# The first S1 group behind the parameter transposes, and whole copies of X chunk 0

## Chip, cores and metric

The kernel runs on one core of one Trainium2 chip. The metric is the device time of one execution in microseconds (us). Most executions of a kernel agree within 0.3%.

## What is computed

A gated mix of two branches over x (2048 tokens, 1024 features, bf16). Cut to what matters:

```python
g = sigmoid((x * gate_w).sum(-1, keepdims=True))
# branch A: a diagonal complex state space model
dt = exp(log_dt); Lam_bar = exp(dt * Lam)
B_bar = ((Lam_bar - 1.0) / Lam)[:, None] * Bmat
h[t] = Lam_bar * h[t-1] + x[t] @ B_bar.T          # over all 2048 tokens
a = 2.0 * real(h @ Cmat.T) + x * Dskip
# branch B: the 8 tokens with the largest x @ w_r go through a gated MLP
b = x + scatter_add(mlp(x_sel) * sigmoid(r_sel))
out = g * a + (1 - g) * b
```

Only the start of branch A is touched by the change: the projection of x by B, and the small parameters (log_dt, Lambda) from which tables of sines and cosines are made.

## The kernel before

**Stages.** Tokens are cut into 8 chunks of 256 (LC); X[m] holds two chunks transposed, features on the partitions. S1 is the projection by B: for each pair of chunks m and each of 8 blocks ct of 128 states, a real and an imaginary group of 8 matmuls accumulate over the features into one PSUM tile "vps" (`s1u`, line 159), and ScalarE evacuates it to V in two casts (`s1e`, line 274, instruction at line 279). There are two vps tiles, so the group (m, ct + 2) needs the evacuation of (m, ct). VectorE turns V by the tables, scans along the tokens and turns back to H (`dve_m`, `dve_scan`, `dve_post`), and S2 multiplies H by C into the output (`s2`, line 757). The MLP of branch B is cut into slots that are put between the S1 and S2 groups.

**Order.** TensorE, VectorE, ScalarE and SP (the queue of most loads) each run their instructions in the order in which the program writes them; the tile framework puts in the semaphore waits. So the order of the lines of the kernel's first part is the order on each engine.

**Loads.** SP's queue issues the first token tile of x (token rows 0 to 127) as it is, then B's first real column block (128 states), x chunk 1 transposed, B's first imaginary block, and the other blocks of B, all transposed by DMA (`load_B`, `load_xT`). ScalarE's queue issues the second token tile (rows 128 to 255), then the three rows log_dt, Lambda_re and Lambda_im into `vrow` (line 85). Chunk 0 of x is not transposed by a DMA but on TensorE: per token tile 8 transposes into the PSUM tile `xq`, and copies from there into X[0] (lines 168 to 174).

**The first part on TensorE, in order.** `warm(12)`: 12 matmuls of zeros (256 columns) into a PSUM tile that nobody reads; the 16 transposes of x chunk 0; `warm(2)`; the first S1 group, `s1u(0, 0, 0, 0, 1)`: state block 0, real part, chunk 0 alone, 8 matmuls of 256 columns; three transposes of the parameter rows into `va_ps` (line 179); `warm(2)`; `s1u(0, 0, 0, 1, 2)`, the same for chunk 1; `s1u(0, 0, 1, 0, 2)`, the imaginary part of both chunks, 8 matmuls of 512 columns; two transposes of the rows w_r and gate_w (line 435); then `s1(0, 1)`, `s1(0, 2)` and so on, 16 matmuls of 512 columns each.

**The parameter chain.** VectorE casts va_ps to `vec` (line 180); ScalarE makes dt_b by an exponential (194); VectorE makes the angles (197) and are (199), ScalarE rdec (201); VectorE makes the arguments of the tables (`tab_arg`, lines 222, 223 and 225, and `tab_abs`, 230); ScalarE the sines and cosines nTi and T2tab (236, 237), three small operations on the angles (393 to 396), and only then the evacuation of state block 0 (279), since `s1e(0, 0)` is written behind them. After it come copies of d0 and two more sines (249, 250), the evacuation of state block 1, and so on.

Lines of the page: L152 is a warm matmul, L164 an S1 matmul, L171 a transpose of x chunk 0, L174 the copies into X[0], L179 the transposes of the parameter rows, L279 the evacuation of V, L298 to L300 the multiplies and adds of `dve_m`, L766 and L782 the S2 matmuls.

Of the kernel before, what the change touches and what calls it, by code (L numbers as in the profile page):

```python
# [10 lines left out]
F32 = mybir.dt.float32  # L11
# [5 lines left out]
P = 128  # L17
LC = 256
# [6 lines left out]
def kernel(  # L25
# [19 lines left out]
    nc = tc.nc  # L45
# [4 lines left out]
    KD = D // P  # L50
# [16 lines left out]
    ps_s1 = ctx.enter_context(tc.tile_pool(name="ps_s1", bufs=2, space=PSUM))  # L67
# [3 lines left out]
    X = {}  # L71
    BT = [const.tile([P, KD, NP_], BF16, name=f"BT{pl}", tag=f"BT{pl}") for pl in range(2)]
# [43 lines left out]
    def big_new(name, k, shape=None, dt=BF16):  # L116
        want = {"V": "H", "U": "U", "H": "V", "D": "V"}[name]
        pick = next((e for e in big_free if e[1] == want), big_free[0])
        big_free.remove(pick)
        big_tag[name, k] = pick[0]  # L120
        return const.tile(shape or [P, 2, NCT, LC], dt, name=name, tag=pick[0])
# [28 lines left out]
    def warm(n):  # L150
        for _ in range(n):
            nc.tensor.matmul(wps[:], lhsT=wt0[:, 0:P], rhs=wt0[:], start=True, stop=True)  # L152

    V = {}
    H = {}

    vp = {}

    def s1u(m, ct, pl, k0, k1):
        if (m, ct) not in vp:  # L160
            vp[m, ct] = ps_s1.tile([P, 2, 2, LC], F32, name="vps", tag="vps")
        o = vp[m, ct][:, pl, k0:k1, :].rearrange("p k t -> p (k t)")
        for dc in range(KD):
            nc.tensor.matmul(o, lhsT=BT[pl][:, dc, ct * P:(ct + 1) * P], rhs=X[m][:, dc, k0 * LC:k1 * LC], start=(dc == 0), stop=(dc == KD - 1))  # L164

    warm(12)
    vec = small.tile([P, 3, NCT], F32, name="vec")
    for tl in range(BPC):
        xq = ps_s2.tile([P, KD, P], BF16, name="xq", tag="zps")
        for dc in range(KD):  # L170
            nc.tensor.transpose(xq[:, dc, :], x0r[:, tl, dc * P:(dc + 1) * P], ident[:])  # L171
        for h, copy in enumerate((nc.vector.tensor_copy, nc.scalar.copy)):
            hs = slice(h * KD // 2, (h + 1) * KD // 2)
            copy(out=X[0][:, hs, tl * P:(tl + 1) * P], in_=xq[:, hs, :])  # L174
    warm(2)
    s1u(0, 0, 0, 0, 1)
    va_ps = ps_m.tile([P, 3, NCT], BF16, name="va_ps", tag="m")
    for i in range(3):
        nc.tensor.transpose(va_ps[:, i, :], vrow[:, i, :], ident[:NCT, :NCT])  # L179
# [59 lines left out]
    def tab_neg(q):  # L239
        cs = slice(q * QC, (q + 1) * QC)  # L240
        nc.vector.tensor_scalar(out=T2tab[:, 1, cs, :], in0=T2tab[:, 0, cs, :], scalar1=-1.0, scalar2=None, op0=ALU.mult)
# [23 lines left out]
    def tab_bwd_b(q):  # L265
        C32, q1, q2 = tabs.pop(q)
        for c in range(QC):
            ct = q * QC + c
            nc.vector.scalar_tensor_tensor(out=Ctab[:, ct, :], in0=C32[:, c, :], scalar=c2r[:, ct:ct + 1], in1=q1[:, c, :], op0=ALU.mult, op1=ALU.add)
            nc.vector.scalar_tensor_tensor(out=S2tab[:, 1, ct, :], in0=C32[:, c, :], scalar=c2i[:, ct:ct + 1], in1=q2[:, c, :], op0=ALU.mult, op1=ALU.add)  # L270
        cs = slice(q * QC, (q + 1) * QC)
        nc.vector.tensor_scalar(out=S2tab[:, 0, cs, :], in0=S2tab[:, 1, cs, :], scalar1=-1.0, scalar2=None, op0=ALU.mult)

    def s1e(m, ct):
        for kk in range(2):
            k = 2 * m + kk
            if k not in V:
                V[k] = big_new("V", k)
            nc.scalar.copy(out=V[k][:, :, ct, :], in_=vp[m, ct][:, :, kk, :])  # L279
        vp.pop((m, ct))  # L280

    def s1(m, ct):
        for pl in range(2):
            s1u(m, ct, pl, 0, 2)
        s1e(m, ct)
# [4 lines left out]
    def bc(ap, c0, c1):  # L290
        return ap[:, c0:c1, :].unsqueeze(1).to_broadcast([P, 2, c1 - c0, LC])

    def dve_m(k, c0, c1):
        v = V[k][:, :, c0:c1, :]
        if c0 == 0:
            G[k] = big_new("U", k)
        u = G[k][:, :, c0:c1, :]
        nc.vector.tensor_tensor(out=u, in0=v, in1=T2tab[:, :, c0:c1, :], op=ALU.mult)  # L298
        nc.vector.tensor_tensor(out=v, in0=v, in1=bc(nTi, c0, c1), op=ALU.mult)  # L299
        nc.vector.tensor_tensor(out=u, in0=u, in1=V[k][:, ::-1, c0:c1, :], op=ALU.add)  # L300
        if c1 == NCT:
            big_done("V", k)
        if k > 0:
            nc.vector.tensor_tensor(out=u[:, :, :, 0], in0=u[:, :, :, 0], in1=rst[k - 1][:, :, c0:c1], op=ALU.add)
# [21 lines left out]
    def dve_p(k, c0, c1, i):  # L326
        if c0 == 0 and i == 0:
            H[k] = big_new("H", k)
        h = H[k][:, :, c0:c1, :]
        g = G[k][:, :, c0:c1, :]  # L330
# [41 lines left out]
    def last_post(hf, c0, c1):  # L372
        k = NK - 1
        if hf == 0 and c0 == 0:
            H[k] = big_new("H", k)
        ts = slice(hf * P, (hf + 1) * P)
        h = H[k][:, :, c0:c1, ts]
        g = G[k][:, hf, :, c0:c1]
# [17 lines left out]
    nc.scalar.activation(out=trig[:, 0], in_=aab[:], func=ACT.Sin, scale=-TWO_PI, bias=halfpi[:])  # L396

    tab_neg(0)
    warm(2)
    s1u(0, 0, 0, 1, 2)  # L400
    s1u(0, 0, 1, 0, 2)
    s1e(0, 0)
# [43 lines left out]
    tab_bwd_q(0, 2, 4)  # L446
    s1(0, 3)
    tab_bwd_b(0)
    dve_m(0, 2, 4)
    dve_scan0(0, 2, 4)  # L450
# [16 lines left out]
    dve_scan0(0, 6, 8)  # L467
    dve_state(0, 4, 8)
    tab_bwd_b(1)
    dve_post(0, 0, 8)  # L470

# [285 lines left out]
    def s2(b, dh):  # L757
# [6 lines left out]
        for ct in range(NCT):  # L764
            for pl in range(2):
                nc.tensor.matmul(zps[:], lhsT=H[k][:, pl, ct, tl * P:(tl + 1) * P], rhs=CT[pl][:, ct, dsl], start=(fresh and ct == 0 and pl == 0), stop=(ct == NCT - 1 and pl == 1), skip_group_check=not fresh)  # L766
        if dh == 1 and tl == 1:
# [126 lines left out]
    for n, (m, k) in enumerate(blocks):  # L894
        free_w.extend(fill.get(n, ()))
        if n == 7:
            for pl in range(2):
                t = const.tile([P, 4, 2, D], BF16, name="wdb", tag=f"BT{pl}")
# [48 lines left out]
```

## Time and profile before

| what | value |
|---|---|
| median of 3 runs | 248.49 us (248.42 to 248.64) |
| profiled execution, time | 248.64 us |
| its span in the profile | 246.9 us |
| granted TensorE clock, mean | 1.00 |
| first token tile of x landed, transposes of x start on TensorE | 4.34, 4.35 us |
| first S1 matmul | 6.75 us |
| parameter rows transposed (va_ps) | 7.89 us |
| vec | 8.16 us |
| first evacuation of V starts | 14.51 us |
| third S1 pair of groups, s1(0, 2), starts | 15.61 us |
| first S2 matmul in the chain | 66.40 us |
| last S2 matmul ends | 243.66 us |

The span is the time from the first to the last record of the profile; the time of the execution holds it and 1.74 us besides. Starts are counted from the span's start. PE is TensorE's matmuls, PEld its weight loads, DVE is VectorE, ACT ScalarE, POOL GpSimd, SP SyncE; a q behind a name is the engine's queue of DMA issues. In a timeline a row has the start, the length, the engine, the line, the operation, the output and input, and in brackets the idle time of the engine ahead of it and what ended that. Matmuls are pipelined, so a row of several is longer than their spacing times their number.

### The profile page before, as it was taken

The numbers are of one execution on the slowest core, as the hardware profiler recorded it, in microseconds if no ns is written. First come the engines' busy times: TensorE is split into PE (matmuls) and PEld (weight loads), VectorE is DVE, ScalarE is ACT, GpSimd is POOL, SyncE is SP. The second block draws the span as 40 slices with busy tenths as digits, with TensorE's granted clock in tenths as the row PEclk, the third lists the DMA queues.
The fourth block names the chain that finished last, engine by engine and source line by source line (L and its number), as shares of the span: only waits on it lengthen the run. The fifth ranks groups of instructions, "written<-read, shape, count | busy, mean of one in ns | idle before, by whom it ended". The sixth has DMA issues, their size and how long they took to land.

```text
span 246.9 us, 3503 instructions
## 1 busy us (share of the span) xinstructions
PE 239.6 (97%) x1354; PEld 112.8 (46%) x1378; DVE 225.9 (92%) x230; ACT 119.2 (48%) x206; POOL 26.8 (11%) x47
## 2 busy tenths in 40 slices
PE   7989999999999999999999999999999999999994
PEld 5534444444444444444444444444444444446453
DVE  0679999999999999999999999999999999999952
ACT  2499994333372563233365472135267445456421
POOL 4000000000000300720002021100000211110210
PEclk9999999999999999999999999999999999999999
DMA  7899999999860270476247989777599999962052
GB/s 185 200 202 200 214 241 208 212 231 262 284 208 0 66 191 0 74 175 212 96 165 221 347 231 353 236 258 279 179 333 303 390 311 305 81 146 39 2 131 85
DMA packets 65313, 48.48 MB, mean 196 GB/s; under 512 B 50560, under 2 KB 52224, under 8 KB 65296
## 3 DMA queue, kind: packets, MB, share of 16 engines
q1 hardware_dynamic: 59968, 37.20, 56.8%
q0 software_dynamic: 3264, 7.38, 14.7%
q10 hardware_dynamic: 2064, 3.68, 4.4%
q8 instruction: 11, 0.18, 0.3%
q14 instruction: 6, 0.05, 0.1%
HBM read 27.55 MB, written 8.40 MB: 146 GB/s over the span
## 4 chain that ended last, share of the span: by engine, by line
PE 93%; DVE 2%; ACT 2%; DMA 1%; issue 1%
PE vps L164 42%; PE zps L766 42%; PE zps L782 3%; PE pgu L658 3%; DMA x0r<-in_A_x_dram 1%; PE y L670 1%; PE xq L171 1%; PE zr L484 1%; DVE tf L225 1%; DVE tu L222 0%; ACT nTi L236 0%; ACT T2tab L237 0%; ACT V L279 0%; DVE tu L223 0%; DVE ot L787 0%
## 5 line engine op out<-in xcount | busy, mean ns | idle before, releaser
L164 PE MATMUL vps<-X,BT 128*128 128x512 bf16 (+1 forms) x508 | 111.7, 376 | 1.7 <-ACT V L279 0.9
L766 PE MATMUL zps<-CT,H 128*128 128x512 bf16 x469 | 104.4, 379 | 0.6
L164 PEld LDWEIGHTS <-BT 128*128 128x128 bf16 x520 | 50.3, 98 | 61.4 <-issue 2.6
L766 PEld LDWEIGHTS <-H 128*128 128x128 bf16 x480 | 46.5, 98 | 56.6 <-issue 1.3
L309 DVE TENSOR_TENSOR_SCAN U<-d,U 128x2048 bf16<-128x2048 f32 (+2 forms) x22 | 62.0, 2859 | 0.6
L279 ACT CAST V<-vps 128x512 bf16<-128x512 f32 x64 | 34.3, 587 | 57.5 <-PE vps L164 55.1
L771 ACT ACTIVATE ot<-zps,gcol 128x512 bf16<-128x512 f32 x30 | 20.6, 686 | 46.1 <-PE zps L766 44.9
L740 ACT CAST zps<-xd 128x512 f32<-128x512 bf16 (+1 forms) x29 | 16.6, 576 | 3.8 <-ACT xt L727 3.3
L299 DVE TENSOR_TENSOR V<-V,nTi 128x4096 bf16<-128x4096 bf16 (+2 forms) x11 | 16.7, 1516 | 0.5
L298 DVE TENSOR_TENSOR U<-V,T2tab 128x4096 bf16<-128x4096 bf16 (+2 forms) x11 | 16.6, 1509 | 0.5
L300 DVE TENSOR_TENSOR U<-U,V 128x4096 bf16<-128x4096 bf16 (+2 forms) x11 | 16.7, 1516 | 0.4
L336 DVE TENSOR_TENSOR H<-H,U 128x4096 bf16<-128x4096 bf16 x7 | 16.0, 2292 | 0.2
L334 DVE TENSOR_TENSOR U<-U,S2tab 128x4096 bf16<-128x4096 bf16 x7 | 16.0, 2292 | 0.2
L792 POOL DMA_DIRECT2D out_dram<-ot x14 | 13.0, 926 | 29.3 <-ACT ot L771 27.3
L704 POOL DMA_DIRECT2D xt<-in_A_x_dram x12 | 7.1, 595 | 82.5 <-DMA out_dram<-xt 36.8
L727 ACT ACTIVATE xt<-xt,omgcol 128x1024 bf16<-128x1024 bf16 x14 | 16.0, 1144 | 0.0
L332 DVE TENSOR_TENSOR H<-U,Ctab 128x4096 bf16<-128x4096 bf16 x7 | 16.0, 2285 | 0.0
L367 DVE TENSOR_TENSOR_SCAN U<-D,U 128x1024 bf16<-128x1024 f32 x4 | 8.9, 2279 | 0.1
L722 DVE TENSOR_TENSOR xd<-xt,Dbc 128x1024 bf16<-128x1024 bf16 x14 | 9.0, 684 | 0.0
L658 PE MATMUL pgu<-wgu,xsel 128*32 128x448 bf16 x128 | 7.2, 354 | 0.1
L782 PE MATMUL zps<-CT,H 128*128 128x256 bf16 (+1 forms) x47 | 7.1, 306 | 0.1
L717 POOL DMA_DIRECT2D out_dram<-xt x2 | 1.5, 754 | 49.2 <-ACT zps L740 49.2
(152 smaller groups left out, 128.3 us busy)
## 6 DMA issues: line engine op xcount, KB each, us to landing
wgu<-in_B_w_gate_dram SPq DMA_DIRECT2D x16, 448.0 KB, 3.6
wgu<-in_B_w_up_dram SPq DMA_DIRECT2D x16, 448.0 KB, 5.7
out_dram<-ot POOLq DMA_DIRECT2D x14, 256.0 KB, 6.4
wdb<-in_B_w_down_dram SPq DMA_DIRECT2D x7, 512.0 KB, 10.7
xt<-in_A_x_dram POOLq DMA_DIRECT2D x12, 256.0 KB, 4.0
out_dram<-xt ACTq DMA_DIRECT2D x12, 256.0 KB, 5.0
wd<-in_B_w_down_dram SPq DMA_DIRECT2D x5, 512.0 KB, 9.9
xt<-in_A_x_dram SPq DMA_DIRECT2D x4, 256.0 KB, 3.3
```

The lines of the kernel that those rows point to most:

```text
L164: nc.tensor.matmul(o, lhsT=BT[pl][:, dc, ct * P:(ct + 1) * P], rhs=X[m][:, dc, k0 * LC:k1 * LC], start=(dc == 0), stop=(dc == KD - 1))
L279: nc.scalar.copy(out=V[k][:, :, ct, :], in_=vp[m, ct][:, :, kk, :])
L298: nc.vector.tensor_tensor(out=u, in0=v, in1=T2tab[:, :, c0:c1, :], op=ALU.mult)
L299: nc.vector.tensor_tensor(out=v, in0=v, in1=bc(nTi, c0, c1), op=ALU.mult)
L300: nc.vector.tensor_tensor(out=u, in0=u, in1=V[k][:, ::-1, c0:c1, :], op=ALU.add)
L309: nc.vector.tensor_tensor_scan(out=fl, data0=d0[:, c0:c1, :].rearrange("p c t -> p (c t)"), data1=fl, initial=0.0, op0=ALU.mult, op1=ALU.add)
L332: nc.vector.tensor_tensor(out=h, in0=g, in1=bc(Ctab, c0, c1), op=ALU.mult)
L334: nc.vector.tensor_tensor(out=g, in0=g, in1=S2tab[:, :, c0:c1, :], op=ALU.mult)
L336: nc.vector.tensor_tensor(out=h, in0=h, in1=G[k][:, ::-1, c0:c1, :], op=ALU.add)
L740: nc.scalar.copy(out=z[:], in_=xd[b][:, d_:d_ + w])
L766: nc.tensor.matmul(zps[:], lhsT=H[k][:, pl, ct, tl * P:(tl + 1) * P], rhs=CT[pl][:, ct, dsl], start=(fresh and ct == 0 and pl == 0), stop= ...
L771: nc.scalar.activation(out=ots[b][:, dsl], in_=zps[:], func=ACT.Copy, scale=gcol[:, b:b + 1])
```

## The change

Two things change; nothing else in the program does.

1. Each token tile of chunk 0 was copied from PSUM into X[0] in two halves, features 0 to 511 by VectorE and 512 to 1023 by ScalarE. Now ScalarE copies the whole of token tile 0, and VectorE the whole of token tile 1.
2. The first S1 group moves on TensorE from ahead of the transposes of the parameter rows to behind them, with one more warm matmul ahead of it. In the program it stands behind `tab_neg(0)`, but no TensorE instruction lies between the parameter transposes and that place, so on TensorE the order is: warm(2), va_ps, warm(1), the first S1 group, warm(2), and on as before. The definition of `s1u` is moved down with it, which has no instruction of its own.

```diff
     warm(12)
     vec = small.tile([P, 3, NCT], F32, name="vec")
     for tl in range(BPC):
         xq = ps_s2.tile([P, KD, P], BF16, name="xq", tag="zps")
         for dc in range(KD):
             nc.tensor.transpose(xq[:, dc, :], x0r[:, tl, dc * P:(dc + 1) * P], ident[:])
-        for h, copy in enumerate((nc.vector.tensor_copy, nc.scalar.copy)):
-            hs = slice(h * KD // 2, (h + 1) * KD // 2)
-            copy(out=X[0][:, hs, tl * P:(tl + 1) * P], in_=xq[:, hs, :])
+        (nc.scalar.copy if tl == 0 else nc.vector.tensor_copy)(out=X[0][:, :, tl * P:(tl + 1) * P], in_=xq[:])
     warm(2)
-    s1u(0, 0, 0, 0, 1)
     va_ps = ps_m.tile([P, 3, NCT], BF16, name="va_ps", tag="m")
...
     tab_neg(0)
+    warm(1)
+    s1u(0, 0, 0, 0, 1)
     warm(2)
     s1u(0, 0, 0, 1, 2)
     s1u(0, 0, 1, 0, 2)
```

More of the change, by code (lines that the diff above doesn't have):

```diff
@@ L152, in warm @@
             nc.tensor.matmul(wps[:], lhsT=wt0[:, 0:P], rhs=wt0[:], start=True, stop=True)
[L154 to L164, printed above, removed]
     warm(12)
@@ L272, in tab_bwd_b, with s1u @@
         nc.vector.tensor_scalar(out=S2tab[:, 0, cs, :], in0=S2tab[:, 1, cs, :], scalar1=-1.0, scalar2=None, op0=ALU.mult)
+    V = {}
+    H = {}
+    vp = {}
+    def s1u(m, ct, pl, k0, k1):
+        if (m, ct) not in vp:
+            vp[m, ct] = ps_s1.tile([P, 2, 2, LC], F32, name="vps", tag="vps")
+        o = vp[m, ct][:, pl, k0:k1, :].rearrange("p k t -> p (k t)")
+        for dc in range(KD):
+            nc.tensor.matmul(o, lhsT=BT[pl][:, dc, ct * P:(ct + 1) * P], rhs=X[m][:, dc, k0 * LC:k1 * LC], start=(dc == 0), stop=(dc == KD - 1))
     def s1e(m, ct):
```

## The prediction

> **What bounds the kernel now.** I read the busy shares first, then the chain of work that ended last, then the waits of TensorE, then the first 24 us instruction by instruction. The first two lines are from the page: TensorE and VectorE are both busy nearly all the time, and the chain is nine tenths TensorE.
>
> ```profile
> PE 239.6 (97%) x1354; PEld 112.8 (46%) x1378; DVE 225.9 (92%) x230; ACT 119.2 (48%) x206; POOL 26.8 (11%) x47
> PE 93%; DVE 2%; ACT 2%; DMA 1%; issue 1%
> ```
>
> So the 2% on VectorE and the 2% on ScalarE are the part of the chain in which TensorE doesn't set the pace. The chain in order of time (start, length, what) shows that they lie in one place, the first 16 us:
>
> ```profile
> 6.27 0.43 DVE X L174
> ...
> 7.36 0.60 PE vps L164 x4
> 7.96 0.17 PE va_ps L179 x3
> 8.13 0.02 issue
> 8.16 0.20 DVE vec L180
> ...
> 14.61 0.96 ACT V L279 x2
> 15.57 0.04 issue
> 15.61 5.45 PE vps L164 x24
> ```
>
> The parameter chain starts with the transposes of the Lambda rows (va_ps), goes over vec, the tables and the sines, and ends with the first evacuation of V on ScalarE (L279), which frees the PSUM tile that the third S1 group needs. From 15.61 us on the chain is TensorE without a break. The waits of TensorE have one entry there (total, times, longest):
>
> ```profile
> PE vps L164 <- ACT V L279: 0.9, 1, 0.9
> ```
>
> So whatever starts the parameter chain earlier moves all that follows, until TensorE's own queue is the later of the two. The timeline gives the pieces (start, length):
>
> ```profile
> 5.42 0.42 DVE L174 COPY X<-xq 128x512 bf16<-128x512 bf16 x1 [4.41 <-PE xq L171]
> 5.88 0.58 ACT L174 COPY X<-xq 128x512 bf16<-128x512 bf16 x1 [2.10 <-DVE X L174]
> 6.03 0.63 PE L152 MATMUL wps<-wt 128*128 128x256 bf16 x2
> 6.27 0.42 DVE L174 COPY X<-xq 128x512 bf16<-128x512 bf16 x1 [0.43 <-PE xq L171]
> 6.73 0.58 ACT L174 COPY X<-xq 128x512 bf16<-128x512 bf16 x1 [0.27 <-DVE X L174]
> 6.75 1.21 PE L164 MATMUL vps<-X,BT 128*128 128x256 bf16 x8
> 7.89 0.23 PE L179 MATMUL va_ps<-ident,vrow 8*128 8x8 bf16 x3
> ```
>
> The first S1 group stands ahead of va_ps on TensorE. It waits for both engines' copies of X, the second ScalarE copy ending at 7.31, and so holds va_ps back to 7.89.
>
> **The change, part by part.** (1) The copies of X chunk 0. Four half copies go (two on VectorE of 0.42, two on ScalarE of 0.58, each of which starts only when VectorE's half of the same tile is done); one whole copy on each engine comes. VectorE's whole copy (1024 elements) has no row. Its bounds are 0.42 and twice that, 0.85. The multiplies of L298 took 0.69 at 1024 elements and 2.29 at 4096, so 0.521 ns per element and 0.156 us fixed; at 512 elements this line gives 0.42, which is the copy's own row, so I take 0.69. ScalarE's whole copy lies between the sine L236 at 1024 elements, 1.06, and two halves, 1.17; I take 1.1. ScalarE may start when VectorE now starts its first half, 5.42, and ends by 6.6. VectorE starts at 6.27 as now (token tile 1 is transposed then) and ends at 6.96, at most 7.12. ScalarE's copy costs nothing, being hidden behind VectorE's by 0.35 us; ScalarE's next work, dt_b, needs vec.
>
> (2) va_ps directly behind the two warm matmuls. These start at 6.03 and 6.24, 0.21 apart, so TensorE is free at 6.45. vec began 0.27 after va_ps's first transpose; that makes about 6.8 with the pause of 0.09 that now stands ahead of va_ps. VectorE is then still in the X copy to 6.96, so vec starts at about 6.99 in place of 8.16: **1.17 us earlier** (1.0 with the copy at 0.85). No DMA is moved, but TensorE reads the rows 1.4 us earlier than now, and their landing isn't shown. The rows ride on ScalarE's queue (q10). Its packets in the windows 4.8 to 5.0 and 5.0 to 5.2 us (packets, MB, share) are the last, none comes from 5.2 to 5.4:
>
> ```profile
> q10 hardware_dynamic: 3, 0.00, 1.4%
> ...
> q10 hardware_dynamic: 1, 0.00, 0.3%
> ```
>
> The same queue's x0r landed at 4.54 (issue 0.74 plus 3.8), some 0.75 to 0.95 after its last large packets near 3.6 to 3.8. By that the rows are there at 5.95 to 6.15, before 6.45. From above the landing is bounded by 7.89, when they are read today without a wait on a DMA.
>
> (3) The first S1 group, now behind va_ps and one more warm matmul. The warm matmul takes 0.11 to 0.21 and lies in the wait for VectorE's copy: nothing; without that wait it would cost its length. The group starts 0.06 after VectorE's copy (as 6.69 to 6.75 now): 7.02. Eight matmuls of 256 columns at 0.107 apart make 7.88; the two warm ones took 0.23 with what follows (8.05 to 8.28): 8.11; the second half, 0.86: 8.97. The imaginary group then needs B's imaginary column block, issued at 5.50 and landed 3.5 later, at 9.0; it began at 9.15 before. So TensorE is 0.10 to 0.15 **ahead** of now, though the group moved behind other work: its own copies come at 6.96 in one piece where they came at 6.69 and 7.31. The pair of groups that follows, (0,1), has 16 matmuls of 512 columns from 11.11 on, 0.215 apart (six steps from 9.37 to 10.66 before it), so it leaves TensorE free at 14.55 now and at about 14.45 afterwards.
>
> (4) What is late next. The chain from vec to L279 has no other input that comes late: the table load follows rdec, the ramp was made at 1.3, and the matmuls that L279 reads are done before 11. So L279 ends at 15.56 - 1.17 = 14.39, and the third pair starts at the later of 14.39 + 0.05 and 14.45: **14.45 for 15.61, 1.16 us earlier**. ScalarE and TensorE then arrive within 0.05 of each other, so any further delay of TensorE in the first 14 us is now paid for. With VectorE's copy at 0.85 it is 1.0; I take 1.1. Behind this point the next meeting is the second evacuation (18.06 to 19.12) with the fourth pair (15.61 + 3.45 = 19.06): both move by the same. VectorE, which waits only 0.9 us for T2tab between vec and the last block, moves by 1.17 too. SP's transposes do not move. The tightest is B imaginary, columns 4 and 5, landed at 17.09 + 5.6 = 22.7; it is read at 19.17 + 3.45 + 1.72 = 24.3 now and 23.2 afterwards, 0.5 to spare. The last two X chunks are issued from 50.43 on in 4.22 us; by the 4.9 us that an earlier one took, the second lands near 57.5, and the gate rows read it at 60.7 now, 59.5 afterwards.
>
> The sum: span 246.9 - 1.1 = 245.8, plus the 1.74 that lie outside the span in the profiled execution (248.64), makes 247.54. That execution is 0.15 above the median of the runs shown, 248.49; against the median it is **247.4 us**, 0.44% less.
>
> [...] Row: the warm matmuls at 6.03 and 6.24 are 0.21 apart, the S1 matmuls from 6.75 on 0.107, so TensorE goes to full speed in between, after 2.4 us of work since 4.35, and the profile's granted clock of 1.0 throughout doesn't show it. [...]
>
> **Rivals.** *The clock comes late* (slower). Place: TensorE between 6.45 and 7.02, where a dense S1 group is replaced by three tiny transposes, a warm matmul and a short pause. Full speed later by t costs t/2, and TensorE has no slack left, so it decides from t/2 = 1.16. [...] Against it: the pause of 0.54 ahead of 4.35 was longer, and only some 0.1 to 0.3 us of work is missing.
>
> *The rows come late* (no change). If they land only near 7.85, va_ps runs when it does today, vec and L279 stay, and TensorE, with two groups behind va_ps, is free at 15.5, just ahead of 15.61: 248.4 us. For it: no row shows the landing; against it: the last packet at 5.2. A landing between gives part of the gain.
>
> *Hidden later.* The gain is real at 14.45 but a transfer that doesn't move takes some back: beyond the 0.5 of B's block the rest would be lost, 248.0 us. Against it: no wait of TensorE on a DMA after 4.35 in the list of waits.
>
> That the change doesn't do what it says can be left aside: program order sets each engine's order here.
>
> **How the numbers follow.** Forecast 0.70 (247.0 to 247.9), late clock 0.16, late rows 0.08, hidden later 0.06. What a measurement can tell is about 0.2%, 0.5 us. Faster by more: the forecast, and half of hidden later, 0.73. Within it: late rows, the other half, and a part of the late clock, 0.13. Slower: the rest of the late clock, 0.14. The range reaches from 247.0 (the 1.17 in full and 0.3 for the spread of the runs shown, 0.22, and what the sum rounds off) over the no-change cases to 248.6.
>
> **What would show it.** vec starting near 7.0 and L279 near 13.35; the third pair near 14.45 with no or a tiny wait on L279; one X copy of about 0.69 on VectorE and 1.1 on ScalarE; S1 matmuls of 256 columns 0.107 apart from 7.0. A va_ps at 7 us or later speaks for late rows; S1 matmuls 0.21 apart after 7 us for the clock; a new wait of TensorE on B or X for the third. The forecast is wrong if the third pair starts later than 15.1, or if it starts near 14.45 and the end doesn't follow.

## The result, and the profile after

| | before | changed |
|---|---|---|
| median, on the same chip | 248.45 us (248.40 to 248.64) | 247.24 us (247.09 to 247.57) |
| ratio | | 0.9952, 95% interval 0.9934 to 0.9969 |
| span of the profiled execution | 246.9 us | 245.8 us |

The changed kernel is 1.2 us (0.5%) faster; the forecast was 247.4. Measured once more on another occasion (r_after below), the medians were 247.52 and 248.32, ratio 0.9975 (0.9958 to 0.9992), 0.8 us apart. Both intervals lie below 1, so there is a gain; by the medians it is 0.8 to 1.2 us. The times themselves spread by about 1 us and more from one execution to the next. The experiments show a part of the reason: neither x nor TensorE's full speed comes at the same moment in every execution. With 12 warm matmuls at the start the transposes of x start at 4.10 to 4.68 us, and full speed, S1 matmuls of 256 columns 0.107 to 0.109 apart instead of 0.21, comes ahead of 4.3 in one profile and only at 10.4 in another.

The profile of the changed kernel numbers its lines otherwise: L160 is the copies into X[0] (L174 before), L164 the transposes of the parameter rows (L179), L165 vec (L180), L269 an S1 matmul (L164), L276 the evacuation of V (L279). From its timeline (start, length, engine, line, operation):

```profile
4.10 1.89 PE L159 MATMUL xq<-ident,x0r 128*128 128x128 bf16 x16 [0.30 <-DMA x0r<-in_A_x_dram]
5.18 1.01 ACT L160 COPY X<-xq 128x1024 bf16<-128x1024 bf16 x1 [1.40 <-PE xq L159]
6.03 0.69 DVE L160 COPY X<-xq 128x1024 bf16<-128x1024 bf16 x1 [5.02 <-PE xq L159]
6.35 0.24 PE L164 MATMUL va_ps<-ident,vrow 8*128 8x8 bf16 x3
6.64 0.17 DVE L165 CAST vec<-va_ps 128x24 f32<-128x24 bf16 x1
6.87 1.03 PE L269 MATMUL vps<-X,BT 128*128 128x256 bf16 x8
9.22 1.41 PEld L269 LDWEIGHTS <-BT 128*128 128x128 bf16 x8 [0.51 <-DMA BT<-in_A_B_im_dram]
9.45 1.67 PE L269 MATMUL vps<-X,BT 128*128 128x512 bf16 x7 [0.46 <-DMA BT<-in_A_B_im_dram]
11.19 13.12 PE L269 MATMUL vps<-X,BT 128*128 128x512 bf16 x59
13.11 1.05 ACT L276 CAST V<-vps 128x512 bf16<-128x512 f32 x2
```

vec starts at 6.64 instead of 8.16, and the first evacuation at 13.11 instead of 14.51. In this execution x landed 0.25 earlier than in the one profiled before (4.10 for 4.35), so 0.25 of the 1.52 is not the change's. The evacuation gains only 1.40; where the other 0.12 went is said under "The parameter chain" below. From 11.19 on TensorE has no pause in the first 24 us: the wait on L279 that set the third pair is gone, and the third pair follows the second at 11.19 + 16 x 0.2157 = 14.64 instead of 15.61. In its place stands a smaller wait, in the list of TensorE's waits (total, times, longest):

```profile
PE vps L269 <- DMA BT<-in_A_B_im_dram: 0.5, 1, 0.5
```

That is the landing of B's first imaginary block: in this execution TensorE is the later of the two, and this block holds it. It landed at 9.18, and the group's eight weight loads start at 9.22. Of its eight matmuls seven are among the records, so the group starts near 9.23 and not at 9.45, 0.4 later than it could have without the wait. In the second profile of the changed kernel (r_after) the block landed at 8.71, and TensorE did not wait for it. The chain of work that ended last shows the block too; in this execution VectorE and ScalarE are gone from its start, and the loads stand there:

```profile
PE 94%; DMA 2%; SPq 2%; issue 1%; DVE 0%
```

### The profile page after: what moved, and what is told of

Read it like the earlier page. It is cut to its first block, busy times and chain, and to the rows that moved or that the text cites. A ratio compares the mean times of both kernels' runs of the same rounds, so it can differ in the third digit from the quotient of the medians.

```text
span 245.8 us, 3504 instructions
## 1 busy us (share of the span) xinstructions
PE 239.3 (97%) x1355; PEld 112.8 (46%) x1379; DVE 225.8 (92%) x229; ACT 119.3 (49%) x205; POOL 26.9 (11%) x47
## 4 chain that ended last, share of the span: by engine, by line
PE 94%; DMA 2%; SPq 2%; issue 1%; DVE 0%
PE vps L269 44%; PE zps L765 42%; PE zps L781 3%; PE pgu L657 3%; DMA BT<-in_A_B_im_dram 2%; PE y L669 1%; SPq L92 1%; PE zr L483 1%; SPq L80 1%; DVE ot L786 0%; SPq L77 0%; PE xselT_ps L570 0%; PE zs_ps L586 0%; PE zt L490 0%; PE vb_ps L434 0%
## 5 line engine op out<-in xcount | busy, mean ns | idle before, releaser
L269 PE MATMUL vps<-X,BT 128*128 128x512 bf16 (+1 forms) x508 | 111.2, 376 | 1.2 <-DMA BT<-in_A_B_im_dram 0.5
L269 PEld LDWEIGHTS <-BT 128*128 128x128 bf16 x520 | 50.2, 98 | 60.3 <-issue 1.0
L276 ACT CAST V<-vps 128x512 bf16<-128x512 f32 x64 | 34.3, 588 | 57.7 <-PE vps L269 55.3
## 6 DMA issues: line engine op xcount, KB each, us to landing
wdb<-in_B_w_down_dram SPq DMA_DIRECT2D x7, 512.0 KB, 10.4
```

## The experiments

Two readings are set against each other throughout. Theory A: the order carries the gain, by an earlier parameter chain, until TensorE's own queue is the later. Rival B: the whole copies carry it.

**One part alone: the order.** The changed kernel, with the half copies put back:

```diff
-        (nc.scalar.copy if tl == 0 else nc.vector.tensor_copy)(out=X[0][:, :, tl * P:(tl + 1) * P], in_=xq[:])
+        for h, copy in enumerate((nc.vector.tensor_copy, nc.scalar.copy)):
+            hs = slice(h * KD // 2, (h + 1) * KD // 2)
+            copy(out=X[0][:, hs, tl * P:(tl + 1) * P], in_=xq[:, hs, :])
```

> The order of the changed kernel (parameter transposes ahead of the first S1 group) with the half copies of before. Theory A (the gain is the parameter chain's earlier start, until TensorE's own queue, now held by B's imaginary block, is the later one): vec can start near 6.7, but dt_b on ScalarE stands behind its second half copy, which ends near 7.3 (7.05 if x lands as early as in the profile of the changed kernel), so the chain starts some 0.3 later than in the changed kernel and L279 ends near 14.5, about level with TensorE; 0.9 to 1.1 us faster than before, 247.4 to 247.6. Rival B (the copies carry the gain): within 0.3 us of before.

Measured: 248.57 us median beside 248.34 of before, ratio 1.0001 (0.9978 to 1.0024), with times from 247.42 to 249.56. The median speaks against theory A, but the times fall apart into two groups, four at 247.4 to 247.6 and seven at 248.6 and up, with one at 248.07 between. The profiled execution (248.58, span 246.8) is one of the upper group. TensorE's timeline there:

```profile
7.29 1.91 PE L271 MATMUL vps<-X,BT 128*128 128x256 bf16 x8
8.99 0.55 PE L152 MATMUL wps<-wt 128*128 128x256 bf16 x2
12.21 4.92 PE L271 MATMUL vps<-X,BT 128*128 128x512 bf16 x22
```

The eight matmuls of the first S1 group take 1.91 us instead of 1.03: they are 0.21 apart, half speed. Its L279 ends at 14.74, but TensorE is free for the third pair only at 12.21 + 3.45 = 15.66. So the chain moved as theory A says, and TensorE lost it again by reaching full speed late. (A smaller part is not its doing: x landed late here, and the transposes of x start at 4.68.) This run alone can't tell what the order is worth.

**The other part alone: the copies.** The kernel before, with the whole copies (the diff above reversed).

> The whole copies of the changed kernel, with the first S1 group ahead of the parameter transposes as before. Theory A: the first S1 group starts as one piece near 7.0 instead of in two at 6.75 and 7.36, so the parameter transposes are 0.0 to 0.15 later than before and the time is 0.0 to 0.15 us longer, 248.4 to 248.6. Rival B: most of the gain is here, 247.3 to 247.6.

Measured: 248.81 us beside 248.34, ratio 1.0017 (0.9993 to 1.0041). No gain is in the copies alone: none of the twelve times lies below 247.90, and rival B expected 247.3 to 247.6, so rival B falls. The median is also above theory A's 248.4 to 248.6. In the chain of the profiled execution (249.53, well above the median) the late full speed shows too, and here it lies on the chain (start, length):

```profile
6.89 1.87 PE vps L164 x8
8.76 0.18 PE va_ps L177 x3
8.96 0.19 DVE vec L178
...
15.41 0.97 ACT V L277 x2
16.38 0.04 issue
16.42 45.16 PE vps L164 x208
```

With the S1 group ahead of the parameter transposes, half speed makes the group 0.84 longer, and the parameters wait for it: vec at 8.96 for 8.16 and the third pair at 16.42 for 15.61.

**The pause on TensorE.** The changed kernel without the warm matmuls around the parameter transposes:

```diff
-    warm(2)
     va_ps = ps_m.tile([P, 3, NCT], BF16, name="va_ps", tag="m")
...
-    warm(1)
     s1u(0, 0, 0, 0, 1)
```

> The changed kernel without the two warm matmuls ahead of the parameter transposes and without the one ahead of the first S1 group: TensorE does almost nothing from 5.8 to 6.9. Theory A (full speed comes from the work done up to about 6, and the landing of the rows is before 6): S1 matmuls of 256 columns 0.107 apart from 6.9, parameter transposes near 6.0 without a wait, time within 0.3 us of the changed kernel, 247.0 to 247.5. Rival C (the pause costs TensorE its full speed): matmuls 0.21 apart for 2 to 5 us after 6.9, TensorE 1.0 to 2.5 us late at the third pair, 248.2 to 249.7. Rival D (the rows land later than 6): the parameter transposes wait for a DMA.

Measured: 248.64 us beside 248.34, ratio 0.9998 (0.9979 to 1.0017): the whole gain is gone. The lines that decide:

```profile
5.96 0.23 PE L163 MATMUL va_ps<-ident,vrow 8*128 8x8 bf16 x3
6.90 1.87 PE L268 MATMUL vps<-X,BT 128*128 128x256 bf16 x8 [0.71 <-DVE vec L164]
```

The parameter transposes run at 5.96 without a wait, so rival D falls. vec starts at 6.67, as in the changed kernel, and L279 ends at 14.06. But after a pause of 0.71 us the S1 matmuls run at half speed (0.21 apart, the group 1.87 long), and the third pair starts at 15.71. Rival C holds in this execution. It was run again on another occasion, to see whether the session or the edit did it:

> The changed kernel without the three warm matmuls around the parameter transposes, once more on another occasion. If the late full speed of its first profile came from the missing warm matmuls, it comes late again: S1 matmuls 0.21 apart from 6.9 to 9 or later, median 248.4 to 248.8, no gain on before. If it came from that session and not from the edit, most times are 247.0 to 247.7, as the changed kernel's.

Measured: 248.60 us beside 248.29, ratio 1.0004 (0.9986 to 1.0022), the S1 group again 1.86 us long:

```profile
7.01 1.86 PE L268 MATMUL vps<-X,BT 128*128 128x256 bf16 x8 [0.71 <-DVE vec L164]
```

So in most executions three matmuls of zeros, that nobody reads, make the difference between a gain of 0.8 to 1.2 us and none: without them 3 of 24 times lie below 247.7, in the changed kernel as it is 11 of 16. The two were not measured on the same occasion; what ties the occasions together is the kernel before, 248.34 and 248.29 beside the runs without them, 248.45 and 248.32 beside the changed kernel. And they are not all that decides, for the order alone keeps the three, and yet its profile has the late full speed and 8 of its 12 times lie above 248.0.

**The changed kernel once more, and the pause ahead of x filled.** The first is the changed kernel as it is. The second has 15 warm matmuls at the start instead of 12, which fill TensorE's wait for x; the third is the kernel before with the same:

```diff
-    warm(12)
+    warm(15)
```

> The changed kernel once more, for its spread beside that of before. Theory F (TensorE goes to full speed at a moment that differs from run to run, 4.7 to 9.4 us in the profiles so far, and the changed kernel has no slack left on TensorE to hide a late one): two groups of times, near 247.1 to 247.5 where it comes by 6.8 and 248.0 to 249.0 where it comes near 9, median between them. Rival (the times of the first four runs hold): all runs 247.0 to 247.7.

> The changed kernel with 15 instead of 12 warm matmuls at the start, so that TensorE has nearly no pause ahead of the transposes of x. [...] Rival (the pause doesn't matter): the same spread as the changed kernel.

> The kernel before with 15 instead of 12 warm matmuls. Theory F: TensorE has 1.0 us of slack there, so the time is that of before within 0.2 us, with fewer runs above 249. Rival (the start of the transposes is delayed): 0.1 to 0.3 longer.

Measured on one chip, before 248.32: the changed kernel 247.52 (246.98 to 249.05), with 15 warm matmuls 247.44 (246.98 to 248.19; ratio to before 0.9967, 0.9952 to 0.9982), the kernel before with 15 248.35 (1.0006, 0.9989 to 1.0023). The changed kernel with 15 on another occasion (below) had 247.50. Filling the pause ahead of x brings nothing that can be measured at the median; the two profiles of the changed kernel with 15 show full speed by 6 us, and the highest of its 23 times is 248.25, while the changed kernel with 12 has one at 249.05, which is too few to call a difference. The two groups of times that theory F expected of the changed kernel are not there either: only one of its times is above 248.1.

**A late full speed, forced.** One warm matmul at the start instead of 12, so that TensorE does nothing until x lands; in the changed kernel and in the one before:

```diff
-    warm(12)
+    warm(1)
```

> The changed kernel with 1 instead of 12 warm matmuls at the start, so that TensorE does nothing until the transposes of x near 4.1 to 4.4. Theory F: full speed comes no earlier than some 7 and up to 11 us, TensorE loses 1 to 2 us more than the changed kernel and has nothing to hide it: 248.3 to 249.8, 1 to 2 slower than the changed kernel's faster runs. Rival (the speed of TensorE in the first 10 us doesn't matter): as the changed kernel.

> The kernel before with 1 instead of 12 warm matmuls at the start; beside the changed kernel with 1 (248.65 us, 0.3 longer than before in its session). Theory G (a late full speed hits both kernels: in the kernel before the slow S1 group ahead of the parameter transposes delays the chain by up to 0.86, in the changed kernel TensorE's own queue is delayed by 1.0 to 1.2): 0.5 to 0.9 longer than before, so the change keeps 0.3 to 0.7 of its gain. Rival H (the kernel before hides it behind its 1.0 us of slack on TensorE, as the prediction had it): within 0.2 of before, and the change's gain is gone when the speed comes late.

Measured: the changed kernel 248.65 beside 248.32 (ratio 1.0017, 1.0004 to 1.0030), the kernel before 249.07 beside 248.23 (1.0028, 1.0019 to 1.0038). Both lose: the changed kernel 1.1 us, the one before 0.8, so the change keeps some 0.4. Theory G holds, H falls. The kernel before, with vec late and TensorE again waiting on L279:

```profile
6.68 1.69 PE L164 MATMUL vps<-X,BT 128*128 128x256 bf16 x8
8.56 0.18 DVE L180 CAST vec<-va_ps 128x24 f32<-128x24 bf16 x1 [1.94 <-PE va_ps L179]
16.02 8.26 PE L164 MATMUL vps<-X,BT 128*128 128x512 bf16 x36 [0.88 <-ACT V L279]
```

and the changed kernel, where L276 starts as early as ever and TensorE's S1 group is what is slow (the profiled execution, 248.01, is the fastest of its twelve, so most lose more than it shows):

```profile
7.02 1.71 PE L269 MATMUL vps<-X,BT 128*128 128x256 bf16 x8
13.13 1.05 ACT L276 CAST V<-vps 128x512 bf16<-128x512 f32 x2
```

**The order alone again, with full speed early.** The first experiment with 15 warm matmuls, and the changed kernel with 15 on the same chip:

> The changed order with the half copies of before, and 15 warm matmuls, so that full speed comes early. Theory A (the order carries the gain, the copies a part of the chain's start): dt_b waits for ScalarE's second half copy, so L279 ends 0.1 to 0.4 later than in the changed kernel, about level with TensorE's own queue: 0.0 to 0.3 longer than the changed kernel with 15, 0.5 to 0.9 faster than before. Rival B (the whole copies carry the gain): as before, 248.3.

> The changed kernel with 15 warm matmuls once more, on the same chip as the two others: 0.6 to 1.0 us faster than before, 247.3 to 247.6, most runs below 247.7.

Measured: 247.80 and 247.50 us beside 248.23, ratios 0.9978 (0.9963 to 0.9994) and 0.9974 (0.9962 to 0.9985). Now the order alone is worth 0.4 us at the median (0.5 by the ratio, the lower end of what theory A expected), and with the whole copies 0.7. By the intervals the two can't be told apart, so the copies' 0.3 is not resolved by the times. The profiles show what the copies do to the chain, but not that it is worth 0.3. The order alone, where dt_b waits for ScalarE's second half copy although vec came at 6.50:

```profile
6.59 0.59 ACT L162 COPY X<-xq 128x512 bf16<-128x512 bf16 x1 [0.21 <-DVE X L162]
7.07 0.21 ACT L181 ACTIVATE dt_b<-vec 128x8 bf16<-128x8 f32 x1
13.33 1.05 ACT L278 CAST V<-vps 128x512 bf16<-128x512 f32 x2
```

With the whole copies dt_b starts at 6.94 although vec comes later, at 6.73, and the evacuation ends 0.13 earlier (14.25 for 14.38). But this does not reach the third pair, which starts at 14.43 with the order alone, set by the evacuation, and at 14.44 with the whole copies, where TensorE is the later. The 0.6 by which the spans differ (246.2 and 245.6) comes from one wait further on, for B's imaginary block of columns 4 and 5, which landed at 23.62 here and at 22.74 there:

```profile
23.66 0.60 PE L271 MATMUL vps<-X,BT 128*128 128x512 bf16 x2 [0.32 <-DMA BT<-in_A_B_im_dram]
```

So the order carries a gain without the copies, and what the copies add to it is not shown.

**What holds TensorE now.** B's imaginary block issued ahead of x chunk 1, chunk 1 in two transposes of 128 tokens, and the groups of state block 0 in the order of landing:

```diff
-    load_xT(1)
     load_B(1, 0, 1)
+    for t in range(2):
+        nc.sync.dma_start_transpose(X[0][:, :, LC + t * P:LC + (t + 1) * P], x2d[LC + t * P:LC + (t + 1) * P, :])
...
     s1u(0, 0, 0, 0, 1)
-    warm(2)
-    s1u(0, 0, 0, 1, 2)
-    s1u(0, 0, 1, 0, 2)
+    s1u(0, 0, 1, 0, 1)
+    for t in range(2):
+        for pl in range(2):
+            for dc in range(KD):
+                nc.tensor.matmul(vp[0, 0][:, pl, 1, t * P:(t + 1) * P], lhsT=BT[pl][:, dc, 0:P], rhs=X[0][:, dc, LC + t * P:LC + (t + 1) * P], start=(dc == 0), stop=(dc == KD - 1))
```

> The changed kernel with B's first imaginary block issued ahead of x chunk 1, chunk 1 transposed by two DMAs of 128 tokens, and state block 0 done in that order (chunk 0 real, chunk 0 imaginary, then each half of chunk 1 real and imaginary; the two warm matmuls between them left out). Theory A (in the changed kernel TensorE, held by the landing of B's imaginary block at 9.2 to 9.45, is what starts the third pair at 14.65, and L279 with its end at 14.16 has 0.45 to spare): after the last landing only 0.9 us of matmuls are left instead of 1.72, the third pair starts 0.3 to 0.5 earlier, 246.7 to 247.0. Rival E (the chain over L279 sets the start in most runs): no difference to the changed kernel, 247.1 to 247.5.

Measured: 248.16 us beside 248.34, ratio 0.9985 (0.9967 to 1.0004), slower than either side expected. Its profiled execution had full speed early, and the third pair did start 0.1 to 0.3 earlier than in the two profiles of the changed kernel, but the loads took it back:

```profile
9.78 1.05 PE L403 MATMUL vps<-X,BT 128*128 128x128 bf16 x16 [0.45 <-DMA X<-in_A_x_dram]
16.41 7.08 PE L270 MATMUL vps<-X,BT 128*128 128x512 bf16 x32 [0.16 <-DMA BT<-in_A_B_im_dram]
23.81 0.39 PE L270 MATMUL vps<-X,BT 128*128 128x512 bf16 x1 [0.32 <-DMA BT<-in_A_B_im_dram]
```

The last part of x chunk 1 lands at 9.7, later than B's block did in the changed kernel (9.18), and TensorE then waits for later imaginary blocks of B, with pauses of 0.16 and 0.32. In this variant an earlier third pair gained nothing, since the loads behind it were not earlier. No variant came out clearly below the changed kernel (247.24 and 247.52); with 15 warm matmuls (247.44 and 247.50) it is level with it.

## Why the prediction was right

**The bound.** All profiles together test the prediction's first claim, that the start of the third pair sets the end. "TensorE free" is the start of the second pair plus 16 x 0.2157, the third pair the later of that and L279's end plus 0.04 to 0.05; us. With 1 warm matmul the first matmul of the second pair is not among the records, and its start is put one spacing ahead of the next.

| kernel | L279 ends | TensorE free | third pair | span | span less third pair |
|---|---|---|---|---|---|
| before | 15.56 | 14.56 | 15.61 | 246.9 | 231.3 |
| changed | 14.16 | 14.64 | 14.64 | 245.8 | 231.2 |
| changed, again | 14.39 | 14.47 | 14.47 | 245.7 | 231.2 |
| changed, 15 warm | 14.02 | 14.24 | 14.24 | 245.7 | 231.5 |
| changed, 15 warm, again | 14.25 | 14.44 | 14.44 | 245.6 | 231.2 |
| before, 15 warm | 14.84 | 13.96 | 14.89 | 246.2 | 231.3 |
| changed, 1 warm | 14.18 | 15.08 | 15.08 | 246.2 | 231.1 |
| before, 1 warm | 15.97 | 14.97 | 16.02 | 247.3 | 231.3 |
| order alone | 14.74 | 15.66 | 15.66 | 246.8 | 231.1 |
| order alone, 15 warm | 14.38 | 14.28 | 14.43 | 246.2 | 231.8 |
| copies alone | 16.36 | 16.12 | 16.42 | 247.7 | 231.3 |
| no warm in between | 14.06 | 15.71 | 15.71 | 246.9 | 231.2 |
| the same, again | 14.18 | 15.96 | 15.96 | 247.1 | 231.1 |
| x chunk 1 split | 13.36 | 14.35 | 14.35 | 246.4 | 232.0 |

The last column is 231.1 to 231.3 in eleven of fourteen, though among these the third pair's start varies by 2.0 us. In the other three TensorE waits for B's imaginary block of columns 4 and 5, which it reads right after its landing: at 23.81 in the split, which has a wait of 0.16 at 16.41 besides, at 23.66 in the order alone with 15, and at 23.14 in the changed kernel with 15.

**The copies.** VectorE's whole copy was put at 0.69 and took 0.69; ScalarE's at 1.1, and took 1.01, hidden as said.

**The parameter chain.** Forecast: vec at 6.99 and the end of L279 at 14.39, for x landing at 4.35. In the second profile of the changed kernel the transposes of x start at the same 4.34, and the evacuation (L276) ends at 14.39. That it fits so closely is luck, for two errors cancel. vec started at 6.87, 0.12 earlier than forecast: its row begins before that of the X copy ahead of it ends (6.95). And from vec to the end of the evacuation it takes 7.52, where the prediction took over the 7.40 of before, since the four multiplies that begin the tables take 1.27 instead of 1.14. The line of before, then three of the changed kernel, again:

```profile
8.90 1.14 DVE L222 TENSOR_SCALAR tu<-ramp,ang 128x256 f32<-128x256 f32 x4
...
6.87 0.17 DVE L165 CAST vec<-va_ps 128x24 f32<-128x24 bf16 x1
7.60 1.27 DVE L207 TENSOR_SCALAR tu<-ramp,ang 128x256 f32<-128x256 f32 x4
13.34 1.05 ACT L276 CAST V<-vps 128x512 bf16<-128x512 f32 x2
```

One of the four rows takes 0.48 instead of 0.35 in five profiles: the four of the changed kernel with 12 and 15 warm matmuls and that of the order alone with 15. In these, and in no other of the fourteen, GpSimd's memset of xsel starts within 0.03 us of that row. That the memset is what slows it was not tested.

The rows of the parameters were said to land by 5.95 to 6.15; the split kernel reads them at 5.47 without a wait on a DMA, so they come earlier than that, and the rival of late rows is out.

**TensorE's queue.** Forecast free at 14.45; 14.47 in the second profile, 14.64 in the first. The term that was off in the first is the landing of B's first imaginary block, put at 9.0: it landed at 9.18, and its group started near 9.23. It was issued 0.48 earlier than in the profile of before and still landed later (9.18 for 8.98); in the second profile it landed at 8.71. That ScalarE and TensorE would meet within 0.05 held in the second profile (14.39 with 0.05 behind it, and 14.47).

**The sum.** 1.1 forecast; the spans of the two profiles are 1.1 and 1.2 shorter than that of before, and the medians 1.2 and 0.8. The 1.1 was read from one execution of before, and a slow one: 248.64, where the kernel's medians are 248.23 to 248.45. The prediction took 0.15 off the level for that, but nothing off the gain. A run of 248.32 has a span of 246.5; with the 231.3 of the table its third pair would start near 15.2, not at 15.61. By this estimate the usual gain is nearer to the 0.8 of the second measurement.

**The rival of the late clock.** Its place was right, the stretch between the transposes of x and 7.02, and its price was real: without the three warm matmuls the S1 matmuls are 0.21 apart for some 3 us from 6.9 on, and TensorE is free for the third pair at 15.71 and 15.96, where the two profiles of the changed kernel have 14.64 and 14.47, 1.1 to 1.5 us later. How late full speed would be was the author's estimate, which no row had shown, and so was the split of this rival's chance between no change and slower. In the changed kernel as it stands a late full speed hardly shows: one of its 16 times lies above 248.1. The warm matmuls that the change keeps and adds have a part in that, for with them taken out the median is 1.1 us higher. What the prediction left out is that a late full speed costs the kernel before as well: there it lengthens the S1 group that stands ahead of the parameters, so the chain is late by 0.8, and the change stays ahead even then (248.65 and 249.07).

When full speed comes is read from the spacing of TensorE's instructions (matmuls of 256 columns 0.21 apart ahead of it, 0.107 to 0.109 behind it). It comes ahead of 4.3 in the split, at 4.5 to 5.9 with 15 warm matmuls, at about 6.5 in the profiles of before and of the changed kernel, at 8.0 and 8.4 with one warm matmul, and at 9.3 to 10.4 with the order alone, the copies alone and without the three warm matmuls. The moment varies even after the same work: the split and the second run without the three warm matmuls had done the same work up to 4.25 (12 warm matmuls, then a pause of 0.45), and one runs its transposes at 0.056 from there on, the other at 0.107, with full speed only at 10.3. What sets the moment no run here shows.

Why it came late in the profiles of the order alone and of the copies alone, which keep their warm matmuls, was not settled. The pauses are a hint. In the four profiles with full speed at 9.3 or later, the pauses that the timeline lists on TensorE between the warm matmuls at the start and the first S1 group add up to 0.77 us or more (0.88 for the order alone, 0.32 and 0.45 for the copies alone, 0.33 or 0.45 and 0.71 without the three); where it came by about 6.5, those ahead of it add up to 0.54 at most. But the kernels with one warm matmul paused for 2.8 us and came to full speed earlier than these four, so this is not the whole of it.

**Hidden later.** It did not happen in the two profiles of the changed kernel, but little is to spare. The block that the prediction named as the tightest, B imaginary, columns 4 and 5, was put at 22.7; it landed there at 22.90 and 22.50, 0.4 and 0.6 ahead of its use. With 15 warm matmuls it came in one profile at 23.09 and took back 0.3, in the order alone with 15 at 23.62 and took back 0.6, and the split gave back 0.8 of its start, most of it there. These loads are the next limit.

## What to carry to other kernels

Ahead of a stream that keeps one engine busy to the end, find the one instruction whose start sets the whole, and write down both of the chains that lead to it: a short chain of small operations may go ahead of a dense group on the shared engine, and pays until the other chain is the later. Here TensorE ran at half speed (matmuls of 256 columns 0.21 us apart instead of 0.107) for the first 4 to 10 us; where the shared engine does that, count the work that keeps it busy as part of the change, since here, in most executions (all but 3 of 24), leaving out three small matmuls of it gave back all that the reordering won. And where the times of one kernel spread by 1 us, compare several profiles by such an anchor, not only medians.

## What was not expected of the hardware

Three matmuls of zeros, some 0.5 us of work, are worth 1.1 us at the median: in the profiles of the changed kernel the S1 matmuls from 6.9 on are 0.109 apart, in the two without the three, after a pause of 0.71, they are 0.21 apart for 3 us. A pause of 0.54 ahead of the transposes of x, in the profiles of before and of the changed kernel again, did not have that effect.

Splitting one PSUM tile's copy between two engines brought no overlap: ScalarE's half starts only when VectorE's half has ended, 0.03 to 0.07 us later, in the five profiles with half copies (in that of before 5.84 to 5.88 and 6.70 to 6.73). One tile for each engine ran at the same time, 5.18 to 6.19 on ScalarE and 6.03 to 6.72 on VectorE.
